# A linear-attention and MLP kernel: whole chunks of 128 tokens in every block, and a planner with other durations

## The chip, the cores and the metric

The kernel runs on one core of a Trainium2 chip. The metric is the time of one execution on the device, in microseconds (us). Before the change the median of three runs is 541.37 us (541.27 to 541.45).

A core has a matrix engine (TensorE, in the profile PE, with its weight loads as PEld), a vector engine (VectorE, DVE), an activation engine (ScalarE, ACT), a general engine (GpSimd, POOL) and a queue that issues transfers (SyncE, SP). Each engine runs its own instructions in the order of the program, and waits for the others by semaphores.

## The reference

Two parts follow each other: a recurrence over 768 tokens for 4 sequences and 8 heads of width 48, with a state of 48 x 48 per head that decays by `w`, and an MLP of 384 - 2048 - 384 over all 3072 tokens.

```python
for t in range(S):                                   # S = 768
    kt, vt, rt, wt = k[:, :, t], v[:, :, t], r[:, :, t], w[:, :, t]
    cur = einsum('bhd,bhe->bhde', u * kt, vt)
    y[:, :, t] = einsum('bhd,bhde->bhe', rt, state + cur)
    state = wt[..., None] * state + einsum('bhd,bhe->bhde', kt, vt)

x = y.transpose(0, 2, 1, 3).reshape(3072, 384)
h = x @ w_in
g = where(h > 0, h, exp(minimum(h, 0)) - 1)
return g @ w_out
```

Everything is in float32. `w` lies between 0.8 and 0.95.

## The kernel before, in words

**Blocks and units.** The tokens are cut into six blocks of 128 tokens of each of the four sequences, so 512 columns of the MLP to a block. The attention of one sequence in one block is a *unit*; unit `i` belongs to block `c = i // 4` and sequence `b = i % 4`.

**The attention of a unit** is the chunked form of the recurrence. Two scans on VectorE (`e_scan` L377, `g_scan` L387) build products of `w` from the end and from the start of the chunk; with them `k` and `r` are scaled (`k_hat` L396, `r_hat` L392). TensorE makes the scores of keys against queries (`score` L456), VectorE copies those under the diagonal into `am` (`mask` L460), whose diagonal was written earlier (`spread`, with the sums of `r*k*u` per head). The output is the sum of the masked scores times the values and of the state times the queries (`value` L501). For the state, TensorE transposes the scaled keys (`trans` L465, copied out by ScalarE L469) and multiplies them with the values (`outer` L532); VectorE scales the state (`scale_state` L472) and adds the products (`update` L540). The output is split into a rounded high part (`x_high` L513) and the rest (`x_low` L519).

**Two kinds of units.** In blocks 0, 1 and 5 a unit is one chunk of 128 tokens. In blocks 2, 3 and 4 (`HALVES`) it is two chunks of 64: the scores are two 64 x 64 squares per head instead of one of 128 x 128, the state is scaled and updated once between the halves, and the TensorE part runs as outer products of both halves (L532), state part of the first half (`state_part` L506), then, after VectorE's update, state part of the second half (L506) and values of both (L493). Where the kind changes, GpSimd rewrites the constants of the scans (`set_reset` L336).

**The MLP of a block** takes 16 slices of 128 of the 2048 inner columns. For each slice, `g1` (L238) makes nine matmuls of 512 columns: three input tiles times three products of high and low parts. ScalarE and VectorE make the activation (`r1` L243, `r2` L246, `stt` L249) and split it (`gh` L253, `gl` L257), and `g2` (L268) makes nine more into the output. In blocks 0 and 1 the first six slices are done in two column halves of 256, since only two of the four units are ready then. In block 0 the weights are also loaded and converted (L559 to L577): they come as eight-byte numbers, of which float32 numbers are put together on VectorE, and split into high and low parts.

**The order of the work** is not written out by hand. Each step is added to a planner (class `Plan`) with its engine, a duration from the table `COST`, the steps that it follows, and for some a due time. `hold` tells which buffers a step takes and who gives them back, by the counts in `SLOTS`: three PSUM banks for attention (`pa`), three buffers for `k` and `r`, one for the transposed keys (`kt`). `order()` first carries the due times backward into a latest time for each step, then plays the program through: whenever an engine is free it takes, of the steps that are ready, the one with the earliest latest time. The instructions are issued in the order that comes out, which is fixed for every engine from then on. Due times come from `BEGINS`, the times at which blocks are to begin: MLP steps are due at an even pace between two of them; the `value` step of a whole unit is due 1 us ahead of its block (with `STAG_C` us between the four), that of a unit in halves 2 us ahead (with `STAG` us between them). Loads of a block are not issued earlier than `LEAD` = 69.5 us ahead of its begin time. `STAY`, `HALF` and `SWITCH` are terms that are zero before the change.

Of the kernel before, what the change touches and what calls it, by code (L numbers as in the profile page):

```python
# [8 lines left out]
F32 = mybir.dt.float32  # L9
# [4 lines left out]
AF = mybir.ActivationFunctionType  # L14
ALU = mybir.AluOpType
# [23 lines left out]
def _pieces():  # L39
    res = []  # L40
    for h in range(H):
        s, e = h * D, (h + 1) * D
        while s < e:
# [7 lines left out]
PIECES = _pieces()  # L51


COST = dict(es=1.5, gs=1.4, pc=0.2, pd=0.6, md=0.22, spa=2.4, rh=0.62, kh=0.62, rk=0.48, rku=0.48, prk=1.1, prku=1.1, dg=0.5, mk=0.7, up=0.7, sc=0.5, xl=0.48,
            cand=0.5, cv=0.9, wl=0.9, stt=0.6, gl=0.64, fl=1.4, kt=0.5, xh=0.46, a=0.87, wh=0.8, r1=0.58, r2=0.6, gh=0.6,
            sp=1.7, s=1.15, t=0.5, v=1.75, v0=1.1, u=0.5, g=2.06, out=0.6, sh=0.6, ya=0.4, vh=1.0)
LAT = 0.06
DMA_FIRST, DMA_ISSUE, DMA_LAT, DMA_RATE = 1.0, 0.45, 1.9, 215.0
BEGINS = (20.9, 120.4, 207.5, 284.8, 361.5, 453.5, 461.1)
SOON = 0.0  # L60
HALF = 0.0
STAY = 0.0
SWITCH = 0.0
MODES = dict(s=1, v=2, u=3, pd=4)
STAG = 10.9
STAG_C = 0.0
HALVES = (2, 3, 4)
FIRST = "DVE"
FILL = {}
COLS = 128  # L70
# [7 lines left out]
class Plan:  # L78
# [5 lines left out]
    def add(self, key, eng, dur, fn, after=(), due=None, start=0.0, lock=False, size=0):  # L84
        self.tasks[key] = dict(key=key, eng=eng, dur=dur, fn=fn, after=list(after), due=due, start=start, lock=lock, size=size)
# [8 lines left out]
    def order(self):  # L94
# [14 lines left out]
        for k in reversed(topo):  # L109
            t = ts[k]  # L110
# [4 lines left out]
        users = {}  # L115
        ring = {p: [0, [False] * n] for p, n in SLOTS.items()}
        free = lambda p, n: not any(ring[p][1][(ring[p][0] + x) % len(ring[p][1])] for x in range(n))
        ready = {e: [] for e in ("PE", "DVE", "ACT", "POOL", "SP")}
        count = {k: len(t["after"]) for k, t in ts.items()}
        at = {k: t["start"] for k, t in ts.items()}  # L120
        rank = {k: n for n, k in enumerate(ts)}
# [2 lines left out]
        server, mode = DMA_FIRST, None  # L124
# [5 lines left out]
        while len(order) < len(ts):  # L130
            moved = False
            for e in ready:
                if busy[e] > now + 1e-9:
                    continue
                best = None
                for k in ready[e]:
                    t = ts[k]
                    if at[k] > now + 1e-9 or any(
                            not free(p, n) or (p in turn and turn[p][0] != k) for p, n, _ in self.holds.get(k, ())):
                        continue  # L140
                    if t["lock"] and max(v for x, v in locked.items() if x != e) > now + 1e-9:
                        continue
                    u = (t["late"] + (STAY if e == "PE" and (k[0] in MODES) != (mode in MODES) else 0.0), rank[k])
                    if best is None or u < best[0]:
                        best = u, k
                if best is None:
                    continue
                k = best[1]
                t = ts[k]
                ready[e].remove(k)  # L150
                for p, n, us in self.holds.get(k, ()):
                    at_, n_ = ring[p][0], len(ring[p][1])
                    ring[p][0] = (at_ + n) % n_
                    for x in range(n):
                        ring[p][1][(at_ + x) % n_] = True
                    if p in turn:
                        turn[p].pop(0)
                        if not turn[p]:
                            del turn[p]
                    h = [p, [(at_ + x) % n_ for x in range(n)], set(us) | {k}]  # L160
                    if p == "pa":
                        for x in us:
                            ts[x]["late"] = min(ts[x]["late"], now + SOON)
                    for x in h[2]:
                        users.setdefault(x, []).append(h)
                end = now + t["dur"] * (2.0 if e == "PE" and now < HALF else 1.0)
                if e == "PE":
                    end += SWITCH * (MODES.get(mode, 0) != MODES.get(k[0], 0))
                    mode = k[0]
                busy[e] = end  # L170
                if t["lock"]:
                    locked[e] = end
                if e == "SP":
                    server = max(server, end) + t["size"] / DMA_RATE / 1e3
                    end = server + DMA_LAT
                t["began"], t["ended"] = now, end
                events.append((end, k))
                order.append(k)
                moved = True
            if moved:  # L180
                continue
            times = [x for x, _ in events] + [v for v in busy.values() if v > now + 1e-9]
            times += [at[k] for e in ready for k in ready[e] if at[k] > now + 1e-9]
            assert times, ("stuck", now, {e: ready[e][:3] for e in ready}, ring)
            now = min(times)
            for end, k in sorted(x for x in events if x[0] <= now + 1e-9):
                events.remove((end, k))
                for h in users.pop(k, ()):
                    h[2].discard(k)
                    if not h[2]:  # L190
                        for x in h[1]:
                            ring[h[0]][1][x] = False
                for s_ in succ[k]:
                    count[s_] -= 1
                    at[s_] = max(at[s_], end + (LAT if ts[s_]["eng"] != ts[k]["eng"] else 0))
                    if not count[s_]:
                        ready[ts[s_]["eng"]].append(s_)
# [94 lines left out]
def rwkv_elu_kernel(ctx, tc, wkr, rk, vp, u, uz, gkrw, gv, gu, w_in, w_out, out):  # L292
    nc = tc.nc
# [16 lines left out]
    tt, stt, act = nc.vector.tensor_tensor, nc.vector.scalar_tensor_tensor, nc.scalar.activation  # L310
# [210 lines left out]
    def outer(u_):  # L521
        v, L = u_["v"], u_["L"]
        if u_["half"]:
            both = [ps_a.tile([P, 512], F32, tag="pa", name="pa_u") for h in range(2)]
            u_["pu"] = [x[:, 0:NP * D].rearrange("d (p e) -> d p e", p=NP) for x in both]
            u_["py"] = [x[:, NP * D:NP * D + NK * HC].rearrange("d (k t) -> d k t", k=NK) for x in both]
        else:
            u_["pu"] = [ps_a.tile([P, NP, D], F32, tag="pa", name="pa_u")]
        for p in range(NP):
            for h, pu in enumerate(u_["pu"]):  # L530
                for z in range(2):
                    nc.tensor.matmul(pu[64 * z:64 * z + D, p], u_["kt"][L * h:L * h + L, p, 64 * z:64 * z + D],  # L532
                                     v[L * h:L * h + L, P * p + 80 * z:P * p + 80 * z + D], start=True, stop=True)
# [39 lines left out]
    def conv_h(f):  # L573
        nc.scalar.copy(w_h[:, f], raws[f][1].bitcast(F32))  # L574

    def conv_l(f):
        tt(w_l[:, f], raws[f][1].bitcast(F32), w_h[:, f].bitcast(F32), ALU.subtract)  # L577

# [18 lines left out]
    for u_ in units:  # L597
# [44 lines left out]
            after.append(("v", i - 1))  # L642
        more = 0.15 * u_["half"]
        if u_["half"]:
            add(("u", i), "PE", K["u"], lambda u_=u_: outer(u_), [("kt", i)] + after[:3])
            add(("ya", i), "PE", K["ya"], lambda u_=u_: state_part(u_, 0), [("u", i), ("sc", i)])
            add(("up", i), "DVE", K["up"], lambda u_=u_: update(u_), [("ya", i)])
            add(("sc2", i), "DVE", K["sc"], lambda u_=u_: scale_state(u_, 1), [("up", i)], lock=True)
            add(("v", i), "PE", K["vh"], lambda u_=u_: value(u_), after + [("sc2", i)], due=BEGINS[c] - (B - 1 - b) * STAG - 2.0)
            add(("up2", i), "DVE", K["up"], lambda u_=u_: update(u_, 1), [("xl", i)])  # L650
        else:
            add(("v", i), "PE", K["v" if c else "v0"], lambda u_=u_: value(u_), after, due=BEGINS[c] - (B - 1 - b) * STAG_C - 1.0 if c > 1 else None)
# [5 lines left out]
    for f in range(NF):  # L658
        for z in range(2):
            add(("raw", f, z), "SP", DMA_ISSUE, lambda f=f, z=z: load_w(f, z), [("raw", f, 0)] if z else [("raw", f - 1, 1)], size=393)  # L660
        add(("a", f), "ACT", K["a"], lambda f=f: conv_a(f), [("raw", f, 0), ("raw", f, 1)])
        add(("cand", f), "DVE", K["cand"], lambda f=f: conv_and(f), [("a", f)], lock=True)
        add(("cb", f), "DVE", K["cv"], lambda f=f: conv_b(f), [("cand", f)], lock=True)
        add(("cc", f), "DVE", K["cv"], lambda f=f: conv_c(f), [("cb", f)], lock=True)
        add(("wh", f), "ACT", K["wh"], lambda f=f: conv_h(f), [("cc", f)])
        add(("wl", f), "DVE", K["wl"], lambda f=f: conv_l(f), [("wh", f)], lock=True)
    n0, prev = 0, None
    seq = []
    for c in range(NC):
# [186 lines left out]
```

## Time and profile before

| What | Before |
|---|---|
| median of 3 runs | 541.37 us (541.27 to 541.45) |
| the profiled execution | 543.14 us |
| its span, first to last instruction | 540.9 us |
| mean granted TensorE clock | 0.974 |
| TensorE busy | 515.5 us, 95% |
| VectorE busy | 371.1 us, 69% |
| ScalarE busy | 285.8 us, 53% |
| GpSimd busy | 74.7 us, 14% |

The profile is of one execution. A group of instructions is named by its line in the kernel, its engine and what it writes from what it reads; "idle before" is the time that the engine stood still just ahead of it, with what ended that. The rows of a timeline give the start of an instruction (or of several alike), its length, and in brackets the idle time ahead of it. Matmuls overlap, so that the length of one is more than its share of time; from the start of one to the start of the next is the better measure. The clock is the share of full speed that TensorE was granted.

The first MLP matmul of the six blocks starts at 26.69, 129.50, 223.98, 306.41, 388.13 and 463.80 us of the span.

### The profile page before, as it was taken

To read this page: it belongs to the slowest core of one execution; us is meant where nothing else is said; L and a number is where in the kernel's file an instruction comes from. 1 tells how busy PE (TensorE), PEld (TensorE's weight loads), DVE (VectorE), ACT (ScalarE), POOL (GpSimd) and SP (SyncE) were. 2 spreads that over 40 slices of the span, in tenths; PEclk is the share of its full clock that TensorE was granted. 3 is DMA by queue.
4 is the path that set the end of the run, shared out by engine and by line. 5 is a ranking of instruction groups with operands and counts; after the bars stand their busy time and mean duration, and the time that the engine had idled before them with its cause. 6 is when DMAs were issued, how large, how long until landed. Compare 5 with 4: busy or idle time off the path is not lost.

```text
span 540.9 us, 12202 instructions
## 1 busy us (share of the span) xinstructions
PE 515.5 (95%) x5121; PEld 427.7 (79%) x5121; DVE 371.1 (69%) x614; ACT 285.8 (53%) x570; POOL 74.7 (14%) x102
## 2 busy tenths in 40 slices
PE   6876999989999999999999999999999999999994
PEld 5666998878999777787777788777788887888883
DVE  5899899988778875469964478964436995333331
ACT  3768588675855453455453365543355543454441
POOL 2000000000243120028120035120031400000000
PEclk9977899979999999999999999999999999999998
DMA  8954754021562200094310083100084110010001
GB/s 243 287 176 141 226 175 164 19 56 35 175 178 76 65 2 2 2 263 133 85 33 2 3 241 103 35 2 3 1 254 124 48 35 2 0 60 0 1 0 63
DMA packets 26749, 47.54 MB, mean 88 GB/s; under 512 B 2753, under 2 KB 9281, under 8 KB 26689
## 3 DMA queue, kind: packets, MB, share of 16 engines
q1 hardware_dynamic: 26544, 46.58, 28.7%
q8 instruction: 42, 0.69, 0.5%
q14 instruction: 19, 0.15, 0.1%
q10 hardware_dynamic: 144, 0.13, 0.1%
HBM read 41.98 MB, written 4.72 MB: 86 GB/s over the span
## 4 chain that ended last, share of the span: by engine, by line
PE 80%; DVE 9%; DMA 6%; ACT 2%; issue 1%; SPq 0%; DVEq 0%; ACTq 0%
PE ph L238 34%; PE acc L268 33%; PE pa_s L456 3%; PE pa_y L501 3%; DMA v<-in_vp_dram 3%; PE pa_u L506 2%; PE pa_u L493 2%; PE pa_u L532 1%; DMA wrawx<-in_w_out_dram 1%; DMA rk<-in_rk_dram 1%; PE pa_t L465 1%; DVE eg L387 1%; DVE gl L257 1%; DMA k<-in_wkr_dram 1%; DVE r L392 1%
## 5 line engine op out<-in xcount | busy, mean ns | idle before, releaser
L243 ACT ACTIVATE m<-ph 128x512 f32<-128x512 f32 (+1 forms) x108 | 59.2, 549 | 132.8 <-PE ph L238 131.5
L249 DVE SCALAR_TENSOR_TENSOR m<-m,ph 128x512 f32<-128x512 f32 (+1 forms) x108 | 67.4, 624 | 84.7 <-ACT m L246 84.2
L238 PE MATMUL ph<-xh,w_h 128*128 128x512 f32 (+1 forms) x324 | 123.2, 380 | 2.0 <-ACT w_h L574 1.6
L238 PE MATMUL ph<-xh,w_l 128*128 128x512 f32 (+1 forms) x324 | 120.7, 372 | 3.7 <-DVE w_l L577 3.7
L268 PE MATMUL acc<-gh,w_h 128*128 128x512 f32 (+1 forms) x325 | 123.6, 380 | 0.0
L268 PE MATMUL acc<-gl,w_h 128*128 128x512 f32 (+1 forms) x325 | 120.2, 370 | 0.1
L238 PE MATMUL ph<-xl,w_h 128*128 128x512 f32 (+1 forms) x324 | 120.1, 371 | 0.0
L268 PE MATMUL acc<-gh,w_l 128*128 128x512 f32 (+1 forms) x325 | 119.9, 369 | 0.0
L257 DVE TENSOR_TENSOR gl<-m,gh 128x512 fp32r<-128x512 f32 (+1 forms) x108 | 73.2, 681 | 36.4 <-ACT gh L253 35.9
L253 ACT CAST gh<-m 128x512 fp32r<-128x512 f32 (+1 forms) x108 | 61.5, 571 | 55.9 <-DVE m L249 33.2
L238 PEld LDWEIGHTS ph<-xh,w_l 128*128 128x128 f32 x324 | 62.3, 192 | 15.0 <-DVE w_l L577 4.6
L238 PEld LDWEIGHTS ph<-xh,w_h 128*128 128x128 f32 x324 | 62.2, 192 | 14.3 <-ACT w_h L574 2.4
L268 PEld LDWEIGHTS acc<-gh,w_h 128*128 128x128 f32 x325 | 62.4, 192 | 12.8 <-issue 1.0
L268 PEld LDWEIGHTS acc<-gh,w_l 128*128 128x128 f32 x325 | 62.4, 192 | 10.2
L268 PEld LDWEIGHTS acc<-gl,w_h 128*128 128x128 f32 x325 | 62.5, 192 | 9.7 <-DVE gl L257 0.5
L238 PEld LDWEIGHTS ph<-xl,w_h 128*128 128x128 f32 x324 | 62.5, 193 | 9.4
L246 ACT ACTIVATE m<-m 128x512 f32<-128x512 f32 (+1 forms) x108 | 63.3, 586 | 2.9
L442 POOL TENSOR_SCALAR_AFFINE_SELECT am<-md 64x256 f32<-64x256 f32 (+1 forms) x56 | 30.5, 548 | 96.9 <-PE pa_u L493 61.9
L404 POOL TENSOR_TENSOR rk<-rk 128x384 f32<-128x384 f32 x16 | 19.1, 1192 | 134.1 <-DMA rk<-in_rk_dram 132.2
L377 DVE TENSOR_TENSOR_SCAN eg<-w,reset 112x516 f32<-112x516 f32 (+1 forms) x24 | 31.0, 1292 | 2.6 <-DMA w<-in_wkr_dram 2.6
L456 PE MATMUL pa_s<-r,k 48*64 48x64 f32 (+1 forms) x576 | 27.3, 262 | 5.5 <-ACT md L425 2.2
L401 ACT ACTIVATE junk<-eg,lim 112x1032 bf16<-112x1032 f32 (+1 forms) x24 | 27.7, 1153 | 8.2 <-DVE eg L387 8.2
(72 smaller groups left out, 513.4 us busy)
## 6 DMA issues: line engine op xcount, KB each, us to landing
v<-in_vp_dram SPq DMA_DIRECT2D x24, 256.0 KB, 6.5
rk<-in_rk_dram SPq DMA_DIRECT2D x16, 384.0 KB, 4.1
w<-in_wkr_dram SPq DMA_DIRECT2D x24, 227.9 KB, 3.9
k<-in_wkr_dram SPq DMA_DIRECT2D x24, 224.0 KB, 4.9
r<-in_wkr_dram SPq DMA_DIRECT2D x24, 224.0 KB, 5.3
out_dram<-o SPq DMA_DIRECT2D x17, 256.0 KB, 2.5
wrawx<-in_w_in_dram SPq DMA_DIRECT2D x10, 384.0 KB, 3.5
wrawx<-in_w_out_dram SPq DMA_DIRECT2D x10, 384.0 KB, 4.1
```

The lines of the kernel that those rows point to most:

```text
L238: nc.tensor.matmul(ph[z:z + COLS], w[:, f, 0, k, z:z + COLS], x_[:, k, :], start=(k == n == 0), stop=(k == NK - 1 and n == 2))
L243: act(s["m"], s["ph"], AF.Relu, scale=-1.0)
L246: act(s["m"], s["m"], AF.Exp, scale=-1.0)
L249: stt_(s["m"], s["m"], -1.0, s["ph"], ALU.add, ALU.max)
L253: nc.scalar.copy(s["gh"], s["m"])
L257: nc.vector.tensor_tensor(s["gl"], s["m"], s["gh"].bitcast(F32), ALU.subtract)
L268: nc.tensor.matmul(a_[z:z + COLS], w[:, f, 1, m, z:z + COLS], g[:, s_], start=(f == n == 0 and lo == 0), stop=(f == NF - 1 and q == parts ...
L377: nc.vector.tensor_tensor_scan(out=eg[:, 0, 0:n][:, ::-1], data0=u_["w"][:, 1:n + 1][:, ::-1], data1=reset[:, 0, 0:n][:, ::-1], initial=0. ...
L401: act(junk[:, :, 0:n], u_["eg"][:, :, 0:n], AF.Relu, bias=lim, accum_out=flags[:, u_["i"]:u_["i"] + 1])
L404: eng.tensor_tensor(u_["rk"][:, 0], u_["rk"][:, 0], u_["rk"][:, 1], ALU.mult)
L442: nc.gpsimd.affine_select(out=am[rs, :, 0:L], in_=u_["md"][rs, q::2].unsqueeze(2).broadcast_to([L, NP, L]), pattern=[[0, NP], [1, L]], com ...
L456: nc.tensor.matmul(pa[q][ts, p, 0:L], u_["k"][rs, p, ts], u_["r"][rs, p, ts], start=True, stop=True)
```

## The change

`HALVES` becomes empty, so that all units are single chunks of 128 tokens: every branch under `u_["half"]` is no longer taken, and no constants of the scans are rewritten. The planner gets other durations; other begin times; a factor of two on TensorE's durations in the first 17 us (`HALF`); a preference of 1 us for staying with attention or with MLP on TensorE (`STAY`); and a time for changes between kinds of matmul (`SWITCH`, `MODES`) and between attention and MLP (`OUTSIDE`). The value steps of the units of blocks 2 to 5 are due 0.2 us apart, 1 us ahead of the block. Another way of converting weights (`BY_DMA`, `conv_n`, `conv_d`, the engine `NET`) is written in but not used, since `BY_DMA` is empty.

```diff
-COST = dict(es=1.5, gs=1.4, pc=0.2, pd=0.6, md=0.22, spa=2.4, rh=0.62, kh=0.62, rk=0.48, rku=0.48, prk=1.1, prku=1.1, dg=0.5, mk=0.7, up=0.7, sc=0.5, xl=0.48,
-            cand=0.5, cv=0.9, wl=0.9, stt=0.6, gl=0.64, fl=1.4, kt=0.5, xh=0.46, a=0.87, wh=0.8, r1=0.58, r2=0.6, gh=0.6,
-            sp=1.7, s=1.15, t=0.5, v=1.75, v0=1.1, u=0.5, g=2.06, out=0.6, sh=0.6, ya=0.4, vh=1.0)
+COST = dict(es=1.3, gs=1.45, pc=0.15, pd=0.95, md=0.15, spa=2.4, rh=0.61, kh=0.61, rk=0.48, rku=0.48, prk=1.0, prku=1.1, dg=0.48, mk=0.65, up=0.72, sc=0.48, xl=0.48,
+            cand=0.5, cv=0.88, wl=0.88, stt=0.6, gl=0.62, fl=1.2, kt=0.45, xh=0.45, a=0.83, wh=0.75, r1=0.57, r2=0.57, gh=0.55,
+            sp=1.6, s=0.95, t=0.4, v=1.6, v0=0.95, u=0.4, uh=0.45, g=2.045, out=0.6, sh=0.55, ya=0.38, vh=0.9)
...
-BEGINS = (20.9, 120.4, 207.5, 284.8, 361.5, 453.5, 461.1)
+BEGINS = (16.3, 114.7, 206.0, 310.0, 397.8, 471.0, 529.3)
 SOON = 0.0
-HALF = 0.0
-STAY = 0.0
-SWITCH = 0.0
-MODES = dict(s=1, v=2, u=3, pd=4)
-STAG = 10.9
-STAG_C = 0.0
-HALVES = (2, 3, 4)
+HALF = 17.0
+STAY = 1.0
+SWITCH = 0.1
+MODES = dict(s=1, v=2, ya=2, u=3, pd=4, t=5)
+OUTSIDE = 0.08
+STAG = 0.0
+STAG_C = 0.2
+BY_DMA = ()
+HALVES = ()
...
                 if e == "PE":
-                    end += SWITCH * (MODES.get(mode, 0) != MODES.get(k[0], 0))
+                    end += SWITCH * (MODES.get(mode, 0) != MODES.get(k[0], 0)) + OUTSIDE * ((mode in MODES) != (k[0] in MODES))
                     mode = k[0]
...
         if u_["half"]:
-            add(("u", i), "PE", K["u"], lambda u_=u_: outer(u_), [("kt", i)] + after[:3])
+            add(("u", i), "PE", K["uh"], lambda u_=u_: outer(u_), [("kt", i)] + after[:3])
...
-        add(("wl", f), "DVE", K["wl"], lambda f=f: conv_l(f), [("wh", f)], lock=True)
+        if f in BY_DMA:
+            add(("wn", f), "ACT", 0.75, lambda f=f: conv_n(f), [("wh", f)])
+            add(("wd", f), "POOL", 1.0, lambda f=f: conv_d(f), [("wn", f)])
+            add(("wl", f), "NET", 4.5, lambda: None, [("wd", f)])
+        else:
+            add(("wl", f), "DVE", K["wl"], lambda f=f: conv_l(f), [("wh", f)], lock=True)
```

More of the change, by code (lines that the diff above doesn't have):

```diff
@@ L117, in order @@
         free = lambda p, n: not any(ring[p][1][(ring[p][0] + x) % len(ring[p][1])] for x in range(n))
-        ready = {e: [] for e in ("PE", "DVE", "ACT", "POOL", "SP")}
+        ready = {e: [] for e in ("PE", "DVE", "ACT", "POOL", "SP", "NET")}
         count = {k: len(t["after"]) for k, t in ts.items()}
@@ L574, in conv_h, with conv_n, conv_d @@
         nc.scalar.copy(w_h[:, f], raws[f][1].bitcast(F32))
+    def conv_n(f):
+        act(w_l[:, f], w_h[:, f].bitcast(F32), AF.Copy, scale=-1.0)
+    def conv_d(f):
+        nc.gpsimd.dma_start(w_l[:, f].bitcast(F32), raws[f][1].bitcast(F32), accum_op=ALU.add)
     def conv_l(f):
```

## The prediction

> **What bounds the kernel now.** I read the page first: the busy shares, the tenths of the clock, the chain that ended last.
>
> ```profile
> span 540.9 us, 12202 instructions
> ...
> PE 515.5 (95%) x5121; PEld 427.7 (79%) x5121; DVE 371.1 (69%) x614; ACT 285.8 (53%) x570; POOL 74.7 (14%) x102
> ...
> PEclk9977899979999999999999999999999999999998
> ...
> PE 80%; DVE 9%; DMA 6%; ACT 2%; issue 1%; SPq 0%; DVEq 0%; ACTq 0%
> ```
>
> TensorE is the bound over the whole, but the clock digits are below 9 only at the front, so the second view was busy time by stage. I cut the span where each block's first MLP matmul starts (26.69, 129.5, 223.98, 306.41, 388.13, 463.8), and asked for two pieces of the first stage.
>
> ```profile
> core 0: us, PE busy (x) PEld busy (x) DVE busy (x) ACT busy (x) POOL busy (x), PEclk, DMA share, GB/s
> 26.69:129.50 102.81, 92.77 (x707) 81.11 (x704) 95.42 (x149) 71.89 (x147) 0.00 (x0) 0.88 0.41 131
> 129.50:223.98 94.48, 94.48 (x1353) 80.40 (x1352) 69.97 (x135) 52.12 (x122) 20.10 (x28) 1.00 0.24 71
> 223.98:306.41 82.43, 81.95 (x1010) 64.97 (x1009) 57.30 (x97) 39.14 (x75) 20.28 (x24) 1.00 0.30 85
> 388.13:463.80 75.67, 75.67 (x568) 61.67 (x567) 49.93 (x72) 36.83 (x66) 14.84 (x16) 1.00 0.28 83
> ```
> ```profile
> 26.69:58.75 32.06, 24.20 (x168) 21.16 (x165) 30.52 (x49) 21.94 (x49) 0.00 (x0) 0.73 0.55 177
> ...
> 112.30:120.20 7.90, 5.72 (x32) 4.67 (x27) 6.81 (x12) 5.19 (x18) 0.00 (x0) 0.57 0.19 50
> ```
>
> There are two regimes. From 129.5 on PE is busy without a break at clock 1.00: what is saved there must be matmul time, and VectorE's work is free (70 of 94, 57 of 82 us). Before 129.5 VectorE is busy 95.42 of 102.81 us (it converts the weights beside the attention), while PE idles 102.81 - 92.77 = 10.0 us and has a mean clock of 0.88. There the order of VectorE's queue decides, and at most its idle 7.4 us can be won: block 1 cannot begin before that work is done.
>
> The third view is the PE timeline of one unit of each kind. Start to next start is the price.
>
> ```profile
> 199.66 0.39 PE L238 MATMUL ph<-xh,w_h 128*128 128x512 f32 x1
> ...
> 201.71 0.55 PE L465 MATMUL pa_t<-ident,k 112*128 112x112 f32 x4
> 202.19 0.69 PE L456 MATMUL pa_s<-r,k 48*64 48x64 f32 x32
> 202.82 0.50 PE L268 MATMUL acc<-gh,w_h 128*128 128x512 f32 x1
> ...
> 205.11 0.57 PE L532 MATMUL pa_u<-v,kt 64*48 64x48 f32 x32
> 205.62 0.54 PE L506 MATMUL pa_u<-r,st 112*32 112x64 f32 x24
> 206.09 0.50 PE L238 MATMUL ph<-xh,w_h 128*128 128x512 f32 x1
> ...
> 208.37 0.54 PE L506 MATMUL pa_u<-r,st 112*32 112x64 f32 x24
> 208.85 0.86 PE L493 MATMUL pa_u<-am,v 64*32 64x64 f32 x64
> 209.63 0.50 PE L268 MATMUL acc<-gh,w_h 128*128 128x512 f32 x1
> ...
> 211.82 0.39 PE L238 MATMUL ph<-xh,w_h 128*128 128x512 f32 x1
> ```
>
> A unit of two 64-token halves costs PE 0.48 (transposes) + 0.63 (scores) + 0.51 (outer products) + 0.47 + 0.47 (state parts) + 0.78 (values) = 3.34 us. It leaves the MLP three times, and the nine MLP matmuls next to it are longer: 2.05 us ahead of the transposes, but 205.11 - 202.82 = 2.29, then 2.28, then 2.19. Against 2.05 that is 0.24 + 0.23 + 0.14 = 0.61. I read 0.14 as the price of coming back from attention and 0.10 as that of going there, except into transposes, where it is nothing. Together 3.95 us a unit.
>
> **The change part by part.** *Blocks 2 to 4, twelve units, become whole chunks on PE.* The trace has such units in blocks 1 and 5.
>
> ```profile
> 122.54 0.55 PE L465 MATMUL pa_t<-ident,k 112*128 112x112 f32 x4
> 123.02 1.16 PE L456 MATMUL pa_s<-r,k 48*128 48x128 f32 x16
> ...
> 153.51 0.56 PE L532 MATMUL pa_u<-v,kt 128*48 128x48 f32 x16
> 154.01 0.60 PE L465 MATMUL pa_t<-ident,k 112*128 112x112 f32 x4
> ```
> ```profile
> 436.46 1.16 PE L456 MATMUL pa_s<-r,k 48*128 48x128 f32 x16
> 437.55 0.86 PE L501 MATMUL pa_y<-r,st 112*32 112x128 f32 x24
> 438.23 1.06 PE L501 MATMUL pa_y<-am,v 128*32 128x128 f32 x32
> 439.22 0.50 PE L238 MATMUL ph<-xh,w_h 128*128 128x512 f32 x1
> ...
> 444.64 0.86 PE L501 MATMUL pa_y<-r,st 112*32 112x128 f32 x24
> ...
> 451.95 0.86 PE L501 MATMUL pa_y<-r,st 112*32 112x128 f32 x24
> ...
> 455.88 0.86 PE L501 MATMUL pa_y<-r,st 112*32 112x128 f32 x24
> ```
>
> Transposes 0.48, scores 437.55 - 436.46 = 1.09, values 0.68 + 0.99 = 1.67, outer products 0.50: 3.74 us, 0.40 more than the halves. Fewer instructions (92 records a unit instead of 180) are dearer, because the scores were 0.63 and are 1.09: the masked half of the square was not computed before. What comes back is crossings. A whole chunk needs two visits (transposes and scores; values and outer products): 0.14 + 0.24 = 0.38, total 4.12, or +0.17 a unit and +2.0 us for twelve. With a third visit for the outer products it is 4.36, +0.41, +4.9 us. If STAY draws the second visit of one unit and the first of the next together, it is one crossing of 0.24: 3.98, +0.03, +0.4 us. I take two visits, +2.0, since the masks on VectorE lie between scores and values in any order.
>
> On the scores the Trainium skill speaks against the change: "TensorEngine Tiling", section Tiling Modes, gives four independent tiles to 64x64 work and two to 64x128, so by it the scores would double, to 1.26 us, and the twelve units cost 2.0 us more than by the rows. The trace agrees in direction and has the price, 1.09.
>
> *VectorE, ScalarE, GpSimd.*
>
> ```profile
> L540 DVE TENSOR_TENSOR st<-st,pa_u 48x192 f32<-48x192 f32 x56 | 19.5, 348 | 6.1 <-PE pa_u L506 5.7
> L472 DVE TENSOR_TENSOR st<-st,pc 112x384 f32<-112x384 f32 x32 | 18.8, 592 | 0.5
> ...
> L460 DVE COPY_PREDICATED am<-upper,pa_s 128x512 f32<-128x512 uint32 x24 | 16.1, 725 | 3.5 <-PE pa_s L456 3.5
> ...
> L460 DVE COPY_PREDICATED am<-upper_h,pa_s 128x256 f32<-128x256 uint32 x24 | 9.3, 439 | 14.3 <-PE pa_s L456 14.2
> ```
>
> Per unit VectorE loses one state scaling (0.59) and two additions (2 x 0.348 = 0.70) and its two masks grow by 0.286 each: -0.7 us. GpSimd loses two resets and has two selects for four. All of this lies beside PE work after 129.5: nothing in time. If that cover were gone, it would still be a gain.
>
> *Order of blocks 0 and 1 (new durations, HALF, STAY, SWITCH, begin times).* No instruction changes here; only the orders do. The cost of one bad place is seen at 112 us:
>
> ```profile
> 110.13 1.84 PE L421 MATMUL pa_d<-ubd,rkc 112*128 112x2 f32 x16
> 111.90 0.56 PE L532 MATMUL pa_u<-v,kt 128*48 128x48 f32 x16
> 114.65 2.08 PE L456 MATMUL pa_s<-r,k 48*128 48x128 f32 x16 [2.18 <-ACT md L425]
> 116.66 0.79 PE L238 MATMUL ph<-xh,w_h 128*128 128x512 f32 x1
> ...
> 120.45 0.39 PE L268 MATMUL acc<-gh,w_h 128*128 128x512 f32 x1
> ```
>
> PE idles 2.18 us; then the granted clock is down (0.57 in 112.3 to 120.2), the scores take 2.01 instead of 1.09 and nine MLP matmuls 3.79 instead of 2.05. One stall costs 2.18 + 0.92 + 1.74 = 4.8 us. "TensorE: Matmul & The Clock Gate" of the Trainium skill (section Part 1, the two states) has the clock fall only after an idle window of some 3.4 us; by it such a stall would cost its 2.2 us alone. The row differs, and decides.
>
> What a better order can win is bounded by VectorE's idle 7.4 us; what a worse one can lose is bounded by no row, and I take one more such stall, +4.8. The durations written in are not all nearer to the rows: the diagonal sums of two units took 111.90 - 110.13 = 1.77, 0.89 each, where the planner had 0.6 and now has 0.95; but the mask goes to 0.65 and the state scaling to 0.48, against 0.725 and 0.592 in the rows above. I take half of the bound, -4 rounded, because VectorE's idle time will not all be reachable by an order.
>
> *Crossings in blocks 1 and 5.* With STAY and OUTSIDE the planner now pays for them. About four fewer at 0.24: -1.0, between 0 and -2.
>
> *Added waits.* Outer products of a whole chunk come after its values; with one buffer for the transposed keys, the next unit's transposes wait for them, and with three key buffers the load of a key three units on waits for those transposes, on SP's queue ahead of later loads. Behind a late one on PE stand all MLP matmuls. I cost this at nothing as long as MLP work of the old block is placed between; the price without that cover is rival one.
>
> **Sum.** -4 + 2.0 - 1.0 = -3.0: a span of 537.9 us. The profiled execution took 543.14 us, 2.24 of it outside its span, and would take 540.1; it stands 1.77 above the median 541.37. Taken from the median: 538.4 us.
>
> **The rivals.** *One, slower: bunching.* The value step was due 10.9 us apart for the four units of a block (2 us ahead of the block); now 0.2 us apart, 1 us ahead. All four units then press into the end of the preceding block, through the single transposed-key buffer, and PE starves where the first MLP step of the next block waits for the fourth unit. It decides if it happens at least once: one stall of 4.8 against the -3.0 gives 543.2; two give 548.0. For it: the chain is new in blocks 2 to 4. Against: block 5 has a common due time already, its values ran at 437.55, 444.64, 451.95 and 455.88, and that stage had PE busy 75.67 of 75.67 us; but its units have no transposes. Chance 0.20.
>
> *Two: the front does not move.* VectorE's order changes, its idle time doesn't. Then +2.0 - 1.0 = +1.0: 542.4; three visits a unit would make it 545.3, one 540.8. For it: 93% busy leaves little. Chance 0.20, of which 0.14 lies within 0.2% of the median (540.3 to 542.5, about what this measurement can tell from no change). The page's price for the scores would bring my own sum to 540.4, to this neighbourhood; it is in that 0.14 with no more weight, since the row has the price.
>
> *Three: more than forecast.* VectorE's 7.4 us all won, one crossing a unit (+0.4), -2.0 in the other blocks: -9.0, 532.4. Chance 0.15.
>
> That the change doesn't do what it says: the general path would run if the decay over 128 tokens passed the guard; blocks 0, 1 and 5 pass it with the same kind of data. I give this nothing.
>
> **The numbers.** Forecast 0.45, from 535.5 to 540.3. Faster 0.45 + 0.15 = 0.60; within 0.2% 0.14; slower 0.20 + 0.06 = 0.26. The range takes in rival three and one stall beyond the no-gain case: 531.5 to 546.5.
>
> **What would show it.** Right: the 64-wide forms of L456, L493, L506 and L532 are gone and PE has about 5121 - 12 x 88 = 4065 records; the stage of a middle block is 82 to 84 us, about what it was; block 1's first MLP matmul comes near 125.5. Wrong: idle PE and a clock below 1.00 after 130 us (rival one); a first MLP matmul of block 1 at 129 or later (rival two); a middle stage under 81 us would say that crossings are dearer than I read them, one over 85 without idle time that there are three visits.

## The result and the profile after

The changed kernel takes 550.88 us (median of 4; 549.55 to 552.03) against 541.41 us in the same runs: a ratio of 1.0165, with a 95% interval of 1.0134 to 1.0195. It is slower by 9.5 us, where 3 us faster was forecast, and lies outside the range of the forecast. The profiled execution took 551.64 us, its span 549.8 us: 8.9 us more than the span before.

The page after:

```profile
span 549.8 us, 9999 instructions
...
PE 513.5 (93%) x4065; PEld 430.9 (78%) x4065; DVE 364.4 (66%) x566; ACT 285.4 (52%) x558; POOL 69.2 (13%) x74
...
PEclk8578699999999999999999999999999998999998
...
PE 78%; DVE 10%; DMA 5%; ACT 3%; issue 2%; SPq 0%; DVEq 0%; ACTq 0%
```

TensorE's records fell to 4065, as counted ahead, and its busy time fell by 2.0 us while the span grew by 8.9: it waits more. Busy time by stage says where; the stages again begin with each block's first MLP matmul, and the columns are those of before.

```profile
34.55:128.64 94.09, 89.16 (x711) 78.53 (x712) 89.04 (x144) 68.23 (x138) 0.00 (x0) 0.91 0.43 134
128.64:228.50 99.86, 97.43 (x1010) 84.31 (x1009) 69.25 (x117) 53.47 (x121) 17.10 (x18) 1.00 0.28 84
228.50:309.64 81.14, 80.20 (x621) 64.90 (x617) 50.58 (x76) 38.97 (x69) 12.90 (x14) 1.00 0.23 67
309.64:393.77 84.13, 81.74 (x660) 66.84 (x656) 54.84 (x80) 39.55 (x71) 19.32 (x16) 1.00 0.27 78
393.77:474.44 80.67, 78.86 (x611) 64.69 (x608) 52.29 (x78) 36.88 (x66) 17.07 (x16) 0.98 0.21 59
474.44:549.80 75.36, 67.90 (x303) 55.87 (x301) 23.53 (x36) 31.77 (x53) 0.00 (x0) 0.97 0.06 23
```

Block 1's first MLP matmul comes at 128.64, 0.86 us earlier than before, so the stage ahead of it lost nothing. Each of the four stages behind it now has PE busy for less than its length: 2.4, 0.9, 2.4 and 1.8 us are missing. As one window, before and after:

```profile
129.50:463.80 334.30, 333.67 (x3936) 272.07 (x3935) 232.67 (x398) 167.63 (x338) 71.94 (x92) 1.00 0.26 76
```
```profile
128.64:474.44 345.80, 338.24 (x2889) 280.73 (x2888) 226.96 (x351) 168.87 (x327) 66.38 (x64) 1.00 0.25 73
```

Idle PE in blocks 1 to 4 was 334.30 - 333.67 = 0.6 us and is 345.80 - 338.24 = 7.6 us. The timeline of PE and of the load queue (SPq) at the end of block 2 shows how it comes about.

```profile
298.04 0.60 PE L467 MATMUL pa_t<-ident,k 112*128 112x112 f32 x4
...
298.68 0.31 SPq L373 DMA_DIRECT2D k<-in_wkr_dram  x1
...
301.43 0.69 DVE L398 TENSOR_TENSOR k<-k,eg 112x512 f32<-112x512 f32 x1
302.34 0.93 PE L458 MATMUL pa_s<-r,k 48*128 48x128 f32 x11
```
```profile
305.38 0.39 PE L270 MATMUL acc<-gh,w_l 128*128 128x512 f32 x1
305.70 0.86 PE L503 MATMUL pa_y<-r,st 112*32 112x128 f32 x24
306.38 1.06 PE L503 MATMUL pa_y<-am,v 128*32 128x128 f32 x32
307.37 0.56 PE L534 MATMUL pa_u<-v,kt 128*48 128x48 f32 x16
307.86 0.60 PE L467 MATMUL pa_t<-ident,k 112*128 112x112 f32 x4
309.14 0.56 PE L534 MATMUL pa_u<-v,kt 128*48 128x48 f32 x16 [0.68 <-ACT kt L471]
309.64 0.50 PE L240 MATMUL ph<-xh,w_h 128*128 128x512 f32 x1
```

The load of the fourth unit's keys is issued at 298.68, just after the transposes of a unit (298.04) have given its key buffer back. Scaling follows at 301.43, scores at 302.34, values at 305.70. By then the last MLP matmul of block 2 (305.38) is gone: PE has only outer products and a transpose to do, waits 0.68 us for ScalarE's copy of the transposed keys, and begins block 3 at 309.64. At the end of block 4 it is worse:

```profile
455.13 0.31 SPq L373 DMA_DIRECT2D r<-in_wkr_dram  x1
...
456.43 0.89 SPq L373 DMA_DIRECT2D k<-in_wkr_dram  x2
...
461.03 1.99 DVE L398 TENSOR_TENSOR k<-k,eg 112x512 f32<-112x512 f32 x2 [1.51 <-DMA k<-in_wkr_dram]
462.09 1.16 PE L458 MATMUL pa_s<-r,k 48*128 48x128 f32 x16 [1.35 <-DVE k L398]
463.67 0.85 PE L534 MATMUL pa_u<-v,kt 128*48 128x48 f32 x16 [0.42 <-DVE xl L521]
464.44 0.80 PE L240 MATMUL ph<-xh,w_h 128*128 128x512 f32 x1
...
467.96 0.38 PE L458 MATMUL pa_s<-r,k 48*128 48x128 f32 x2
```

Here the last key loads (456.43) stood in the queue behind a load of `r` that could be issued only at 455.13, after 6.1 us of waiting for values. VectorE waits 1.51 us for these keys, and TensorE has two waits, 1.35 us for VectorE's scaling and 0.42, and then nine MLP matmuls that take 467.96 - 464.44 = 3.52 us.

In the planner this is the difference. In a unit of two halves, transposes and outer products lead to the unit's own values, so they inherit the values' latest time. In a whole chunk the outer products only lead to the state of the next block: their latest time, and that of the transposes, lies a block later. Among ready steps the planner takes the one with the earliest latest time, so MLP steps go first, and the transposes, which give the key buffers back, stay behind. The rows show how late that can be. The second unit of block 1 is a whole chunk in both kernels; here are its values and its outer products, before and after:

```profile
126.32 1.06 PE L501 MATMUL pa_y<-am,v 128*32 128x128 f32 x32
...
140.99 0.56 PE L532 MATMUL pa_u<-v,kt 128*48 128x48 f32 x16
```
```profile
125.11 1.09 PE L503 MATMUL pa_y<-am,v 128*32 128x128 f32 x32
...
200.47 0.56 PE L534 MATMUL pa_u<-v,kt 128*48 128x48 f32 x16
```

The outer products came 15 us behind the values before, and come 75 us behind them now.

### The profile page after: what moved, and what is told of

It is laid out like the page before. It is cut to its first block, busy times and chain, and to the rows that moved or that the text cites. A ratio compares the mean times of both kernels' runs of the same rounds, so it can differ in the third digit from the quotient of the medians.

```text
span 549.8 us, 9999 instructions
## 1 busy us (share of the span) xinstructions
PE 513.5 (93%) x4065; PEld 430.9 (78%) x4065; DVE 364.4 (66%) x566; ACT 285.4 (52%) x558; POOL 69.2 (13%) x74
## 4 chain that ended last, share of the span: by engine, by line
PE 78%; DVE 10%; DMA 5%; ACT 3%; issue 2%; SPq 0%; DVEq 0%; ACTq 0%
PE ph L240 33%; PE acc L270 32%; PE pa_y L503 5%; PE pa_s L458 4%; DMA k<-in_wkr_dram 2%; DVE gl L259 1%; PE pa_u L534 1%; DVE k L398 1%; PE pa_t L467 1%; DVE r L394 1%; DMA wrawx<-in_w_out_dram 1%; DMA v<-in_vp_dram 1%; DVE m L251 1%; DVE eg L389 1%; DVE am L462 1%
## 5 line engine op out<-in xcount | busy, mean ns | idle before, releaser
L270 PE MATMUL acc<-gh,w_h 128*128 128x512 f32 (+1 forms) x325 | 121.4, 374 | 0.1
L259 DVE TENSOR_TENSOR gl<-m,gh 128x512 fp32r<-128x512 f32 (+1 forms) x108 | 71.5, 666 | 39.6 <-ACT gh L255 38.8
L458 PE MATMUL pa_s<-r,k 48*128 48x128 f32 x384 | 31.9, 304 | 14.0 <-ACT md L427 8.9
L458 PEld LDWEIGHTS pa_s<-r,k 48*128 48x128 f32 x384 | 26.6, 204 | 21.4 <-ACT md L427 9.6
L462 DVE COPY_PREDICATED am<-upper,pa_s 128x512 f32<-128x512 uint32 x48 | 32.4, 729 | 13.8 <-PE pa_s L458 13.6
L444 POOL TENSOR_SCALAR_AFFINE_SELECT am<-md 128x512 f32<-128x512 f32 x32 | 28.9, 926 | 93.1 <-PE pa_y L503 93.1
```

The costliest lines, as they stand in the source:

```text
L259: nc.vector.tensor_tensor(s["gl"], s["m"], s["gh"].bitcast(F32), ALU.subtract)
L270: nc.tensor.matmul(a_[z:z + COLS], w[:, f, 1, m, z:z + COLS], g[:, s_], start=(f == n == 0 and lo == 0), stop=(f == NF - 1 and q == parts ...
L444: nc.gpsimd.affine_select(out=am[rs, :, 0:L], in_=u_["md"][rs, q::2].unsqueeze(2).broadcast_to([L, NP, L]), pattern=[[0, NP], [1, L]], com ...
L458: nc.tensor.matmul(pa[q][ts, p, 0:L], u_["k"][rs, p, ts], u_["r"][rs, p, ts], start=True, stop=True)
L462: nc.vector.copy_predicated(u_["am"][q][:, :, 0:L], upper_h4 if u_["half"] else upper4, u_["pa"][q][:, :, 0:L])
```

## The experiments

Three theories were named first. **W**: the idle time comes from the late latest times of transposes and outer products. **B**: it comes from the value steps of a block being due together. **P**: it comes from the planner's new numbers, and the length of the chunks has no part in it. Idle PE is measured in every run as above, from block 1's first MLP matmul to block 5's. The kernel before, run beside them, took 541.98 us (beside e1 to e4), 541.72 (e5 to e8) and 541.69 (e9 to e11).

| Run | us | ratio to before (95%) | idle PE, us |
|---|---|---|---|
| e1 old planner, whole chunks | 561.32 | 1.0365 (1.0327 to 1.0403) | 13.5 |
| e2 after, values staggered | 558.86 | 1.0334 (1.0286 to 1.0381) | 10.7 |
| e3 after, halves | 551.58 | 1.0201 (1.0160 to 1.0242) | 6.5 |
| e4 after, outer products due | 543.93 | 1.0036 (1.0007 to 1.0066) | 1.2 |
| e5 as e4, begin times chosen anew | 540.58 | 0.9974 (0.9951 to 0.9996) | 0.6 |
| e6 halves, begin times chosen anew | 547.46 | 1.0093 (1.0056 to 1.0130) | 7.8 |
| e7 as e4, without 8.9 us of VectorE work | 540.44 | 0.9972 (0.9951 to 0.9994) | 2.9 |
| e8 after, two buffers of transposed keys | 549.93 | 1.0143 (1.0105 to 1.0181) | 7.8 |
| e9 as e1, outer products due | 538.32 | 0.9942 (0.9916 to 0.9968) | 0.2 |
| e10 as e3, outer products due | 550.69 | 1.0173 (1.0123 to 1.0224) | 6.4 |
| e11 after, outer products due late | 556.67 | 1.0292 (1.0239 to 1.0346) | 9.7 |

**e1: one half of the change alone**, the kernel before with whole chunks.

```diff
-HALVES = (2, 3, 4)
+HALVES = ()
```

> The kernel before with whole chunks in every block and nothing else changed. Theory W (TensorE waits at the ends of blocks, because the transposes and outer products of a whole chunk have their latest time a block later and keep the key buffers): idle PE of 7 us or more after block 0, 548 to 560 us. Theory P (the planner's new numbers make the waits, chunk length is innocent): 541 to 544 us. Theory B (value steps due all at one time): as W, since the due times of whole chunks lie together here too.

561.32 us, beyond even W's range. With the old numbers the same picture is more plain: at the end of block 2, transposes and outer products alternate, and each outer product waits for ScalarE's copy of the keys just transposed.

```profile
305.41 0.55 PE L465 MATMUL pa_t<-ident,k 112*128 112x112 f32 x4
306.57 0.56 PE L532 MATMUL pa_u<-v,kt 128*48 128x48 f32 x16 [0.62 <-ACT kt L469]
307.07 0.60 PE L465 MATMUL pa_t<-ident,k 112*128 112x112 f32 x4
308.35 0.56 PE L532 MATMUL pa_u<-v,kt 128*48 128x48 f32 x16 [0.68 <-ACT kt L469]
308.85 0.60 PE L465 MATMUL pa_t<-ident,k 112*128 112x112 f32 x4
310.13 0.56 PE L532 MATMUL pa_u<-v,kt 128*48 128x48 f32 x16 [0.68 <-ACT kt L469]
```

P's claim that chunk length has no part falls. Without a due time for the outer products the new numbers are the better ones for whole chunks, 551 us against 561; with one it is the other way round (e4 and e9 below).

**e2: the values staggered.**

```diff
-STAG_C = 0.2
+STAG_C = 10.9
```

> The changed kernel with the value steps of a block due 10.9 us apart instead of 0.2. Theory B: idle PE after block 0 falls from 7.6 to under 2 us, 543 to 545 us. Theory W: the key buffers still wait for late transposes, idle stays at 5 to 10 us, 548 to 556 us.

Slower, with 10.7 us idle instead of 7.6. B falls. The time and the idle time are both a little beyond W's range.

**e3: the other half alone**, the new planner with halves.

```diff
-STAG = 0.0
+STAG = 10.9
...
-HALVES = ()
+HALVES = (2, 3, 4)
```

> The changed kernel with halves again in blocks 2 to 4, due 10.9 us apart as before; durations, terms and begin times stay the new ones. Theory P: still slower than before, 547 us or more. Theory W: transposes and outer products of halves lead to the unit's own values and come early, so blocks 3 and 4 end without idle PE: 541 to 547 us.

551.58 us: within P's range and not W's. But all of the waits of more than 0.3 us lie between 214 and 231 us, at the end of block 1, whose own units are whole chunks; the ends of blocks 2 and 3 have none, as W has it. The outer products of block 1 ran at 139.18, 179.74, 191.11 and 201.46 us here, and at 137.75, 140.99, 153.51 and 159.95 before, with the same kinds of units and the same rule in the planner's code. So that rule lets the planner put them late and doesn't force it; which of the new numbers tips it wasn't tried. Whether the waits here are theirs is asked by e10.

**e4: a due time for the outer products**, the one added thing.

```diff
-            add(("u", i), "PE", K["u"], lambda u_=u_: outer(u_), [("kt", i), ("v", i)])
+            add(("u", i), "PE", K["u"], lambda u_=u_: outer(u_), [("kt", i), ("v", i)], due=BEGINS[c] - 6.0 + 8.0 * b if c > 0 else None)
```

> The changed kernel with one thing added: the outer products of blocks 1 to 4 get a due time of their own near their block's begin (from 6 us ahead of it, 8 us apart), and with them the transposes. Theory W: idle PE after block 0 falls from 7.6 to 3 us or less, 544 to 547 us. Theories B and P: nothing that they name changes, 549 to 552 us.

543.93 us, and the idle time falls from 7.6 to 1.2 us:

```profile
131.69:466.60 334.91, 333.75 (x2846) 276.70 (x2845) 221.47 (x342) 164.76 (x314) 65.96 (x64) 1.00 0.26 75
```

W's idle time is met, and its time but for 0.1 us. Against the changed kernel it is 7 us less, for 6.4 us less idle time. What is left against the kernel before lies ahead of block 1, whose first MLP matmul stands at 131.69 instead of 129.50; from there to the end the span is 542.1 - 131.69 = 410.4 us, where it was 411.4.

**e5: whole chunks without waits.** The due time again (7.4 us ahead, 13.1 apart), and begin times, `STAG_C`, `STAY`, `LEAD`, `SOON` and `LAT` chosen anew, so that the planner's order holds no idle PE behind block 0.

```diff
-BEGINS = (16.3, 114.7, 206.0, 310.0, 397.8, 471.0, 529.3)
+BEGINS = (23.2, 114.7, 204.3, 307.5, 406.5, 481.0, 486.8)
```

> Whole chunks in every block, outer products with a due time of their own as in the run before, and begin times, STAY, LEAD and LAT chosen so that the planner's own order has no idle TensorE after block 0. Theory W (the loss is idle TensorE): idle PE after block 0 under 1.5 us, and what is left against the kernel before is the matmul price of whole chunks, about +1.3: 540 to 544 us. Rival C (whole chunks cost something beside the waits): 546 us or more, without idle PE.

540.58 us, idle 0.6 us: W, and rival C falls. Whole chunks without waits are slightly faster than the kernel before.

**e6: halves with numbers chosen anew** in the same way, by begin times, `STAG`, `STAG_C`, `STAY`, `LEAD`, `SOON` and `LAT`.

```diff
-HALVES = ()
+HALVES = (2, 3, 4)
...
-BEGINS = (16.3, 114.7, 206.0, 310.0, 397.8, 471.0, 529.3)
+BEGINS = (23.2, 129.5, 217.3, 263.3, 264.6, 439.9, 455.0)
```

> The changed kernel with halves again in blocks 2 to 4, begin times and the other numbers of the planner chosen so that its order has no idle TensorE there. Theory W: the slow run with halves came from waits at one block end, so without them 538 to 542 us, 0 to 3 us under the tuned whole chunks. Theory P (the new durations and terms are bad for halves): 546 us or more.

547.46 us, P's number; but the run has 7.8 us of idle PE that the planner's order didn't hold (between 146 and 154, between 202 and 226, and at 331 us), so the condition of the test wasn't reached, and it decides nothing between W and P. (In this order the second scan of unit 6 runs after the constants were rewritten for halves, so with constants that aren't its own; the steps and their sizes are the same.)

**e7: less work on VectorE in the front.**

```diff
-        add(("cand", f), "DVE", K["cand"], lambda f=f: conv_and(f), [("a", f)], lock=True)
-        add(("cb", f), "DVE", K["cv"], lambda f=f: conv_b(f), [("cand", f)], lock=True)
+        add(("cb", f), "DVE", K["cv"], lambda f=f: conv_b(f), [("a", f)], lock=True)
```

> The kernel with due outer products, with the 16 mask operations on VectorE in the conversion of the weights left out (0.55 us each, 8.9 us; the weights are wrong then). Theory F (before block 1 VectorE sets the pace, as the prediction had it): the first MLP matmul of block 1 comes 5 to 9 us earlier than 131.7 us, 535 to 539 us in all. Rival G (arrival of weights, TensorE's own chain and its clock set the pace there): it moves by less than 3 us, 541 to 545 us.

The kernel leaves out the 16 mask operations of the conversion, so its weights are others than the reference's. Block 1's first MLP matmul stands at 131.56 us, against 131.69 in e4: rival G by the mark that was set. Yet block 0's last `g2` begins at 129.41 instead of 133.85, 4.4 us earlier, and the time, 540.44, is 3.5 us less than e4's in spite of a new wait of 2.15 us, and between the two ranges. So VectorE's work seems to be part of what holds the front, but much less than what is taken off it comes out. Neither theory holds as stated.

**e8: two buffers of transposed keys.**

```diff
-            hold("kt", ("t", i), [("u", i)])
+            if c == 0:
+                hold("kt", ("t", i), [("u", i)])
+            else:
+                hold("wg", ("t", i), [("u", i)], fifo=False)
```

From block 1 on `trans_out` takes its tile from that ring of two, which the conversion of the weights no longer needs by then.

> The changed kernel with two buffers for the transposed keys from block 1 on (the conversion's, free by then), the order of the steps the same. Theory W (late latest times, not the buffer): idle PE stays near 7 us, 548 to 552 us. Rival K (the single buffer makes the waits, as the prediction's first rival had it): idle falls to 3 us or less, 543 to 547 us.

549.93 us, idle 7.8 us. Rival K, the single buffer, falls for the changed kernel: a second buffer alone changes nothing. It wasn't tried on e1, where transposes and outer products alternate.

**e9: the due time with the old planner**, on e1.

```diff
-HALVES = (2, 3, 4)
+HALVES = ()
...
-            add(("u", i), "PE", K["u"], lambda u_=u_: outer(u_), [("kt", i), ("v", i)])
+            add(("u", i), "PE", K["u"], lambda u_=u_: outer(u_), [("kt", i), ("v", i)], due=BEGINS[c] - 6.0 + 8.0 * b if c > 0 else None)
```

> The kernel before with whole chunks in every block (561 us in the first call) and the due time of the outer products added (6 us ahead of the block's begin, 8 us apart); all other numbers of the planner are the old ones. Theory W: the 13.5 us of idle PE after block 0 fall to 2 us or less, 541 to 546 us. Rival: the old numbers do not fit whole chunks at all, whatever the outer products' due time, 552 us or more.

538.32 us: 23 us less than e1 by one due time, better than expected, and the fastest of all. Idle PE is 332.01 - 331.83 = 0.2 us; at the end of block 2 outer products now follow values, and MLP matmuls stand behind them.

```profile
128.24:460.25 332.01, 331.83 (x2844) 275.72 (x2843) 219.96 (x346) 166.17 (x324) 68.80 (x64) 1.00 0.25 76
```
```profile
297.13 1.06 PE L501 MATMUL pa_y<-am,v 128*32 128x128 f32 x32
298.12 0.56 PE L532 MATMUL pa_u<-v,kt 128*48 128x48 f32 x16
298.61 0.50 PE L268 MATMUL acc<-gh,w_h 128*128 128x512 f32 x1
...
300.79 0.39 PE L238 MATMUL ph<-xh,w_h 128*128 128x512 f32 x1
```

**e10: the due time on e3**, where only block 1 has whole chunks. Its edit is e3's with the line of e4.

> The kernel with halves in blocks 2 to 4 under the new numbers (551.6 us in the first call), with the due time of the outer products added, which here reaches only the whole units of block 1. Theory W: the waits ahead of block 2 (6.5 us between 214 and 231) go to 1 us or less; if no others come up elsewhere, 542 to 545 us. Rival (they come from the halves' own longer chain under the new numbers): they stay, 549 to 553 us.

The waits at the end of block 1 are gone, as W has it. Others came up, most of them at the ends of blocks 2 and 3 (1.41 us at 392.98 the longest), and the time, 550.69, is hardly less and in the rival's range. So the waits of e3 were those of block 1's whole chunks; why halves wait at the later ends under the new numbers wasn't taken apart.

**e11: the due time 26 us later.**

```diff
-            add(("u", i), "PE", K["u"], lambda u_=u_: outer(u_), [("kt", i), ("v", i)])
+            add(("u", i), "PE", K["u"], lambda u_=u_: outer(u_), [("kt", i), ("v", i)], due=BEGINS[c] + 20.0 + 8.0 * b if c > 0 else None)
```

> The changed kernel with the same due time for the outer products, but 26 us later (20 us behind the block's begin, 8 us apart). Theory W: late outer products bring the waits back, 7 us or more of idle PE after block 0, 549 to 558 us. Rival (any due time would have done, by shaking up the order): 541 to 546 us.

556.67 us with 9.7 us idle. It isn't that any due time makes the order a better one: an early one helps, and this late one doesn't.

```profile
129.78:479.41 349.63, 339.93 (x2890) 280.12 (x2889) 223.86 (x351) 168.38 (x327) 63.40 (x64) 1.00 0.25 72
```

What stays open is whether halves, freed of waits under the new numbers, would do as well as whole chunks, since neither e6 nor e10 got there.

## Why the prediction was wrong

**What bounds the kernel: right, with a gap.** Behind 129.5 us only PE time counts. That holds after too; what the prediction did with it was to price PE's busy time and take the absence of idle time for granted, because before had none there.

**The front, -4.0: it gave -0.9.** The stall at 112 us did go, as the step supposed, but the first MLP matmul came 7.9 us later (34.55 after 26.69). Most of that is one wait. ScalarE's copy of the diagonal sums, on which the first scores wait, stood at 12.47 us before (first row); now it stands behind a step of the conversion that waits 6.46 us for weights, and the first scores begin at 21.12 instead of 14.64.

```profile
12.47 0.14 ACT L425 COPY md<-pa_d 128x8 f32<-128x8 f32 x1
```
```profile
18.26 0.89 ACT L561 ACTIVATE wg<-wrawx 128x768 f32<-128x768 f32 x1 [6.46 <-DMA wrawx<-in_w_out_dram]
...
21.12 0.80 PE L458 MATMUL pa_s<-r,k 48*128 48x128 f32 x2 [7.12 <-ACT md L427]
```

The bound by VectorE's idle time was the wrong measure as well: e7 took 8.9 us of work off VectorE, and block 1 didn't begin earlier. What sets its begin instead stays open, and the clock can't settle it: the changed kernel and e8 have spans of 549.8 and 549.6 us at granted clocks of 0.959 and 0.994, but at the start the clock that is shown doesn't tell the pace (last section).

**Units and crossings, +2.0 and -1.0: the sum about right, in part by luck.** From block 1's first MLP matmul to the end the span grew from 540.9 - 129.50 = 411.4 to 549.8 - 128.64 = 421.2 us, by 9.8. Idle PE is 6.9 of it. At the lowered clock at 464 us nine MLP matmuls took 3.52 us instead of some 2.2 and an outer product 0.77 instead of 0.50, 1.6 together. The rest, 9.8 - 6.9 - 1.6 = 1.3 us, is left for the price of whole chunks less crossings; the forecast had +1.0. The single prices were kept (values 307.37 - 305.70 = 1.67, outer products 0.49). But the visits to attention, counted in the timeline from 133 us on, fell from 51 to 25, by 26 where the forecast had about 16. Taken from start to start without idle time, the MLP matmuls from block 1 on went from 340.9 to 338.9 us, 1.3 of it at the lowered clock, so that the 26 visits saved some 3.4 us, 0.13 each instead of 0.24. A count that was too low and a price that was too high made up for each other. In e9, with 39 visits and no waits, whole chunks even come out ahead.

**Added waits, at nothing: the step that failed.** The prediction saw the chain: the next unit's transposes wait for the outer products, and a key load three units on waits for those transposes. It put it at zero "as long as MLP work of the old block is placed between", and didn't ask what the planner would place there. The answer was in the code: with `u` following `v`, nothing in the block asks for `u`. Idle PE grew by 6.9 us and the lowered clock took 1.6, together 8.5 of the 8.9 us by which the span grew. The single waits end on different things (VectorE's masks, its scaled keys and its `gl`, ScalarE's copy), so the rows alone don't tie each of them to the late transposes; that a due time for the outer products took 6.4 us of the idle time away, with the clock at 1.00, does it for most (e4).

**Rival one, with 0.20, named the right effect and the wrong cause.** PE does starve where the next block waits for the fourth unit. But not because the values are due together (e2 made it worse), nor through the single buffer (e8 made it no better). Its price was also off: it had one or two stalls of 4.8 us, where there were thirteen waits of 0.2 to 1.35 us, and the clock fell after one pair only. Its evidence against, block 5 with common due times, was weak for the reason that stood beside it: those units have no transposes.

## What to carry to other kernels

When a change lets a step lead somewhere else, ask what now makes a list scheduler want it: a step whose results are needed late may be put late, even if it holds the buffers that the next work waits for. A due time for the step that gives a buffer back may be worth more than the buffer (e4 and e9 against e8). And when the engine that bounds a kernel shows no idle time before a change, price its waits after it all the same, since an order written for other dependencies has to earn that again.

## What the runs showed of the hardware

The granted clock didn't follow every wait. Behind a single wait of 1.55 us (e2, at 353 us) and in the stretch of several short ones in the changed kernel (208 to 229 us, 1.8 us of idle PE in all) it stayed at 1.00; behind one of 2.15 us (e7, at 360 us) it was at half for some 3.4 us, and so it was behind the pair of 1.35 and 0.42 us in the changed kernel. The nine MLP matmuls behind these waits agree: 355.44 - 353.17 = 2.27 us in e2, 363.74 - 360.01 = 3.73 in e7, 3.52 behind the pair. "TensorE: Matmul & The Clock Gate" of the Trainium skill (Part 1) has it fall after an idle window of some 3.4 us; here less was enough, and the rows decide.

```profile
353.17:360.00 6.83, 6.83 (x78) 5.40 (x82) 6.23 (x10) 3.14 (x6) 1.39 (x3) 1.00 0.14 36
```
```profile
208.43:229.00 20.57, 18.75 (x333) 15.02 (x333) 14.88 (x29) 8.42 (x16) 3.62 (x4) 1.00 0.46 141
```
```profile
360.01:364.00 3.99, 3.99 (x11) 3.13 (x12) 3.96 (x6) 2.91 (x6) 0.00 (x0) 0.57 0.00 0
```

At the start the clock that the profile shows and the pace of the matmuls part. In e8 the 16 matmuls of the diagonal sums took 3.81 us at 8.59 us, with the clock shown as 1.00, and 1.84 us at 114.96. The runs don't show why.

```profile
8.59 3.81 PE L423 MATMUL pa_d<-ubd,rkc 112*128 112x2 f32 x16 [2.52 <-DVE rkc L418]
```
```profile
8.59:12.40 3.81, 3.73 (x16) 3.56 (x16) 2.23 (x4) 1.12 (x2) 0.00 (x0) 1.00 1.06 296
```
